# A routing search fed by two broadcasting transfers instead of sixteen, and four weight buffers that outlive the attention

## The chip, the cores and the metric

The program runs on one core of one Trainium2 chip. The metric is the device time of one execution in microseconds (us), lower is better. TensorE (PE) multiplies matrices and loads its weights in a part of its own (PEld), VectorE (DVE), ScalarE (ACT) and GpSimd (POOL) do the rest of the arithmetic, and SyncE (SP) issues transfers (DMAs), which run on 16 DMA engines.

## The reference

Three stages follow each other, all in float32 except the weights of the third.

```python
thresh = np.max(scores, axis=-1, keepdims=True) - tau          # 4 x 8 heads, 576 x 576 scores, head_dim 64
scores = np.where(scores >= thresh, scores, -1000000000.0)
...
attn = np.exp(scores) / sum
x = (attn @ v) as [2304 tokens, 512]

logits = x @ w_gate                                            # 8 experts, cap = 2304 // 8 = 288
for idx in np.argsort(-logits.flatten()):                      # greedy, with capacity
    tok, e = idx // 8, idx % 8
    if assigned[tok] >= 0 or counts[e] >= cap: continue
    assigned[tok] = e; counts[e] += 1
out[mask_e] = np.maximum(x[mask_e] @ w1[e], 0) @ w2[e]         # 512 -> 1024 -> 512

gate = 1 / (1 + np.exp(-(x @ w_gate2)))                        # 512 -> 1536, weights are float64 words
return gate * (x @ w_val) @ w_out                              # 1536 -> 512
```

The third stage's weights arrive as 64-bit floats, and the kernel turns them into 32-bit floats by integer operations on their two halves.

## The kernel before

**Attention** (0 to 344 us) works through 16 units of two heads in an order written out by hand. Beside it, a "fill" generator puts small work into gaps: the class `Narrow` loads raw pieces of the third stage's weights (36 pieces, three for each of 12 column blocks: gate, val, out; one raw piece is a tile `wd` of 128 x 1024 words, 512 KB), makes float32 of each in three DVE operations (`n1`, `n2`, `n3`, at L585, L587, L589) in a tile `wn`, and stores it to device memory (`wf<-wn`, 256 KB). 13 pieces are done in the attention, through four `wd` buffers and three `wn` buffers. Those pools end with the attention.

**Routing** is done by rounds: in each, every token that is left picks its best expert, and for each expert a threshold is searched that lets no more in than there is room. Rounds 0 to 2 search by `search` (L639 to L719: compare a tile `big`, count by 18 short matmuls L684, a flag `fl` L699, one matmul L702, a new value `n` L705; six such steps). Rounds 3 to 6 search by `search_wide`: the 8 x 2304 keys are written to device memory (`kx<-kc`) and read back in two halves `kw`, each of 128 partitions by 1152 keys, so that 16 partitions hold the same row of one expert. One step is then one DVE comparison with a count for each half (`big<-kw`, L765), a flag `rhw` (L768), and one matmul (L771). In the kernel before, each half is read by eight transfers of 16 partitions.

**Experts.** For each of the eight experts the tokens are gathered, transposed (L1190), multiplied by w1 and w2 (expert 0 in float32, L1241 and L1264; the others in two parts, L1146 and L1156, with weights that ACT and DVE split into a high and a low part from `wr`, L1227 and L1054, three `wr` buffers), and put through the third stage (L1146, L1156, called stage g below, from the parts `yh`, `yl`), whose result is transposed back (L1377), copied (`orow`, L1384) and scattered to the output. Round r+1 of the routing runs beside expert r.

The third stage's 36 weight pieces are made ready beside this, once, in rounds 0 and 1: pieces narrowed before come from device memory (`wf<-wf`, L1069), the others are loaded raw (`wd`, L1078) and narrowed on DVE (L1087, L1090, L1093, again n1 to n3). ACT and DVE then split each (`hi` L1110, `lo` L1054, names `wgh`, `wgl`, `wvh`, `wvl`, `wo`).

What sets the order: `Plan` is a list scheduler that runs while the program is built. Each piece of work is a `job` with an engine, a cost, what it depends on, a priority and the buffers that it takes (`Slots`). `Plan.step` places, on the engine that is free first, the job of the lowest priority number that is ready; while `crit` (the next step of round 0) is known, only jobs that end before it are put in front. The costs thus decide the order of instructions on every engine, and the chip then runs each engine's list in that order. All loads and stores stand in one list on SP: a transfer that waits holds up all behind it. A job of a DMA is taken to end after its bytes at 300 KB/us plus 1.9 us.

Of the kernel before, what the change touches and what calls it, by code (L numbers as in the profile page):

```python
# [7 lines left out]
F32 = mybir.dt.float32  # L8
F32R = mybir.dt.float32r
BF = mybir.dt.bfloat16  # L10
I32 = mybir.dt.int32
# [97 lines left out]
def n_pieces():  # L109
    return len(fill_places()) // 3  # L110


def fill(router, weights, slots):

    it = router
    next(it)
    for slot in range(slots):
        weights.load(slot)
    yield
    for _ in it:  # L120
        pass
    yield
    yield from weights.steps()


def attention(tc, raw, prep, qk, v, tau, wg, xd, lg, idf, filler, chosen):
# [402 lines left out]
T, E, CAP, R = 2304, 8, 288, 96  # L529
# [35 lines left out]
class Narrow:  # L565
# [10 lines left out]
            self.d[n] = self.raw(self.todo.pop(n))  # L576
            (q or self.q).dma_start(self.d[n], self.src[n])

    def steps(self):
        v = self.nc.vector  # L580
        for n, slot in self.slots.items():
            f = self.narrowed(n)
            w = self.d.pop(n).rearrange("p (n t) -> p n t", t=2)
            o = f.bitcast(I32)
            v.tensor_scalar(o, w[:, :, 1], 3, 0x3FFFFFF8, op0=OP.logical_shift_left, op1=OP.bitwise_and)  # L585
            yield n
            v.scalar_tensor_tensor(o, w[:, :, 0], 29, o, op0=OP.logical_shift_right, op1=OP.bitwise_or)  # L587
            yield n
            v.scalar_tensor_tensor(o, w[:, :, 1], -0x40000000, o, op0=OP.bitwise_and, op1=OP.bitwise_or)  # L589
            self.store(n, f)  # L590
            self.load(slot)
            yield n + 1


class Router:
# [136 lines left out]
    def search_wide(self, K, C):  # L732

        nc, v = self.nc, self.nc.vector
        yield "DVE", 1.0
        kc = self.t([128, 8, 18], "kc")
        no = self.t([128, 8, 18], "no")
        ct = C.rearrange("p c e -> p e c")
        v.tensor_tensor(kc, ct, K.unsqueeze(1).to_broadcast([128, 8, 18]), op=OP.mult)
        v.tensor_scalar(no, ct, -3 * DEAD, 3 * DEAD, op0=OP.mult, op1=OP.add)  # L740
        v.tensor_tensor(kc, kc, no, op=OP.add)
        rem = self.t([128, 2, 8], "remw")
        for i, col in enumerate((C_NM, C_M)):
            v.tensor_tensor(rem[:, i], self.rem, self.cf[:, col : col + 8], op=OP.add)
        yield "SP", 0.35
        nc.sync.dma_start(self.kx.rearrange("e p c -> p e c"), kc)
        for h in range(2):
            yield "SP", 2.7, "kw2" if h else "kw"
            for e in range(8):
                nc.sync.dma_start(  # L750
                    self.kw[h][16 * e : 16 * e + 16],
                    self.kx[e : e + 1, 64 * h : 64 * h + 64].rearrange("a p c -> a (p c)").to_broadcast([16, T // 2]),
                )
        w = None
        for s, sh in enumerate(range(28, -1, -4)):
# [24 lines left out]
        self.close(w, ps, nf)  # L780
# [143 lines left out]
class Plan:  # L924
# [76 lines left out]
    def place(self, t, j):  # L1001
# [12 lines left out]
        if more:  # L1014

            self.dma = max(self.dma, t + j.dur) + more / 300e3
            j.end = self.dma + 1.9
        self.done.append((t, j))
        for h in (*j.acq, *j.use):
            h.left -= 1  # L1020
# [2 lines left out]
                h.pool.free.append((h.end, h.slot))  # L1023


def experts(tc, rt, xd, idf, w12, w3in, w3, pre, out):
    nc = tc.nc
    V, A, G, SP = nc.vector, nc.scalar, nc.gpsimd, nc.sync
    with (
# [13 lines left out]
        p = Plan()  # L1043
# [4 lines left out]
        pos_g = [32 + 52 * e for e in range(7)] + [32 + 52 * 6 + 36]  # L1048

        def bt(h, shape, name, dt=F32):  # L1050
            return bp.tile(shape, dt, name=name, tag=f"b{h.slot}")

        def minus(l, x, h):
            V.tensor_sub(l, x, h.bitcast(F32))  # L1054
# [4 lines left out]
        for n in range(36):  # L1059
# [13 lines left out]
            else:  # L1073
# [4 lines left out]
                    SP.dma_start(box["w"], w3in[n])  # L1078
                    return 524288

                src = job("SP", 0.35, load, (), pr - 60, acq=[hd, hc])

                def n1(box=box):
                    box["f"] = wp.tile([128, 512], F32, name="wf", bufs=NWF)
# [7 lines left out]
                def n3(box=box):  # L1092
                    V.scalar_tensor_tensor(box["o"], box["w2"][:, :, 1], -0x40000000, box["o"], op0=OP.bitwise_and, op1=OP.bitwise_or)  # L1093

                src = take = job("DVE", 0.36, n1, [src], pr, acq=[hf] + hold, use=[hd, hc])
                src = job("DVE", 0.63, n2, [src], pr, use=[hd, hc, hf])
                src = job("DVE", 0.63, n3, [src], pr, use=[hd, hc, hf])
            if kind == 2:
                take.order = taken[-1:]
                taken.append(take)  # L1100
# [398 lines left out]


NEAR = 40
PATIENT = 2.0, 30.0
START, SPACE = 5.5, 1.7
WD, NWF, LEAD, LATE, PB, WIDE, AHEAD = 4, 3, 14, 3, 18, 3, 40
PLANS = []


# [13 lines left out]

def program(tc, qk, v, tau, wg, w12, cst, csti, w3, out):
    nc = tc.nc
    with tc.tile_pool(name="keep", bufs=1) as kp, tc.tile_pool(name="keep_dram", bufs=1, space=bass.MemoryType.DRAM) as dp:
        idf = kp.tile([128, 128], F32, name="idf")
        make_identity(nc, idf)
        lg = kp.tile([128, 18, 8], F32, name="lg")
        xd = dp.tile([2304, 512], F32, name="xd")
        wf = [dp.tile([128, 512], F32, name=f"wf{n}") for n in range(36)]
        words = w3.bitcast(I32)  # L1530
        rt = Router(tc, lg, idf, kp, dp)
        pre = n_pieces()
        with (
            tc.tile_pool(name="at_raw", bufs=2) as rp, tc.tile_pool(name="at_prep", bufs=2) as pp,
            tc.tile_pool(name="staging", bufs=2) as sp,
        ):
            weights = Narrow(
                nc, lambda s: sp.tile([128, 1024], I32, name="wd", bufs=4), lambda n: sp.tile([128, 512], F32, name="wn", bufs=3),
                words, nc.sync, lambda n, f: nc.sync.dma_start(wf[n], f), {n: n % 4 for n in range(pre)},
            )  # L1540
            filler = fill(rt.prepare(cst, csti), weights, 4)
            attention(tc, rp, pp, qk, v, tau, wg, xd, lg, idf, filler, rt.begin)
        experts(tc, rt, xd, idf, w12, words, wf, pre, out)


# [12 lines left out]
```

## Time and profile before

| | |
|---|---|
| median of 3 runs | 1127.85 us (1127.82 to 1128.93) |
| the profiled execution | 1127.83 us |
| its span, first to last instruction | 1126.0 us, so 1.8 us lie outside |
| mean granted TensorE clock | 0.977 |
| PE busy, PEld busy | 1055.1 us (94%), 983.5 us (87%) |
| DVE, ACT, POOL busy | 787.3, 525.4, 324.2 us |
| DMA | 156.17 MB, mean 139 GB/s |

The shares are averages over a part with a PE bound (the attention and the experts), a part of 40 us in which PE is idle most of the time (344 to 384 us, round 0 of the routing), and some short stops. What a change is worth has to be read at the place where it acts.

### The profile page before, as it was taken

To read this page: it belongs to the slowest core of one execution; us is meant where nothing else is said; L and a number is where in the kernel's file an instruction comes from. 1 tells how busy PE (TensorE), PEld (TensorE's weight loads), DVE (VectorE), ACT (ScalarE), POOL (GpSimd) and SP (SyncE) were. 2 spreads that over 40 slices of the span, in tenths; PEclk is the share of its full clock that TensorE was granted. 3 is DMA by queue.
4 is the path that set the end of the run, shared out by engine and by line. 5 is a ranking of instruction groups with operands and counts; after the bars stand their busy time and mean duration, and the time that the engine had idled before them with its cause. 6 is when DMAs were issued, how large, how long until landed. Compare 5 with 4: busy or idle time off the path is not lost.

```text
span 1126.0 us, 21012 instructions
## 1 busy us (share of the span) xinstructions
PE 1055.1 (94%) x7885; PEld 983.5 (87%) x7885; DVE 787.3 (70%) x1915; ACT 525.4 (47%) x1176; POOL 324.2 (29%) x334
## 2 busy tenths in 40 slices
PE   4999999999994699998999999999999999999997
PEld 3888888888883479997999999999999899999996
DVE  7899999989997998876868857966974413412311
ACT  4798898889873234234125214314313413412411
POOL 5888998888840101011011010110101100100101
PEclk9999999999996799998999999999999999999999
DMA  7423334244016675646346346446444433534232
GB/s 277 153 86 111 132 100 142 89 143 128 2 38 220 201 275 174 225 122 191 95 125 199 120 122 187 134 136 169 149 124 153 134 113 114 166 105 125 76 108 84
DMA packets 52885, 156.17 MB, mean 139 GB/s; under 512 B 11568, under 2 KB 16560, under 8 KB 50864
## 3 DMA queue, kind: packets, MB, share of 16 engines
q1 hardware_dynamic: 49712, 145.40, 40.3%
q0 software_dynamic: 3072, 9.44, 2.8%
q8 instruction: 62, 1.02, 0.4%
q14 instruction: 39, 0.32, 0.1%
HBM read 135.38 MB, written 19.43 MB: 137 GB/s over the span
## 4 chain that ended last, share of the span: by engine, by line
PE 51%; issue 26%; DVE 14%; DMA 4%; ACT 2%; POOL 2%; SPq 0%; POOLq 0%; ACTq 0%; DVEq 0%
PE ps L1146 17%; PE acc L1156 11%; PE s L250 7%; PE t L291 5%; PE o L367 2%; PE o L391 2%; DVE nm L261 2%; PE o L363 2%; PE o L375 2%; DMA wr<-in_w 2%; DVE p L283 1%; DMA wf<-wf 1%; POOL out L1388 1%; DVE wf L1090 1%; DMA wd<-in_w 1%
## 5 line engine op out<-in xcount | busy, mean ns | idle before, releaser
L1332 DVE TENSOR_TENSOR gt<-ps,sg 128x288 f32<-128x288 f32 x96 | 43.9, 457 | 163.0 <-PE ps L1146 128.8
L1388 POOL DMA_INDIRECT out<-orow,idx x24 | 24.4, 1017 | 410.0 <-ACT orow L1384 405.9
L1328 ACT ACTIVATE sg<-ps 128x288 f32<-128x288 f32 x96 | 39.5, 412 | 195.1 <-PE ps L1146 170.5
L1156 PE MATMUL acc<-gh,wo 128*128 128x288 f32 x768 | 125.1, 300 | 0.9 <-DVE wo L1054 0.9
L265 ACT ACTIVATE e<-s,nm 128x576 f32<-128x576 f32 x144 | 106.4, 739 | 24.9 <-DVE nm L261 23.4
L1054 DVE TENSOR_TENSOR w<-wr,w 128x512 fp32r<-128x512 f32 x112 | 75.6, 689 | 55.7 <-ACT w L1227 55.3
L1146 PE MATMUL ps<-yh,wgh 128*128 128x288 f32 x384 | 107.9, 303 | 6.3 <-ACT orow L1384 3.9
L1336 ACT ACTIVATE gh<-gt 128x288 fp32r<-128x288 f32 x96 | 42.7, 445 | 148.1 <-DVE gt L1332 144.6
L283 DVE SCALAR_TENSOR_TENSOR p<-s,th,e 128x576 f32<-128x576 f32 x128 | 100.7, 810 | 15.5 <-ACT th L269 13.3
L1156 PEld LDWEIGHTS acc<-gh,wo 128*128 128x128 f32 x768 | 108.8, 189 | 1.2 <-DVE wo L1054 1.1
L261 DVE TENSOR_REDUCE nm<-s 128x1 f32<-128x576 f32 x144 | 104.1, 747 | 6.1 <-PE s L250 5.1
L1171 POOL DMA_INDIRECT xr<-xd,idx x16 | 15.2, 951 | 321.4 <-issue 157.2
L1146 PE MATMUL ps<-yh,wvh 128*128 128x288 f32 x384 | 106.4, 299 | 0.0
L1146 PE MATMUL ps<-yh,wgl 128*128 128x288 f32 x384 | 106.3, 298 | 0.0
L1227 ACT ACTIVATE w<-wr 128x512 fp32r<-128x512 f32 x112 | 69.0, 629 | 77.4 <-PE acc L1156 30.1
L1146 PE MATMUL ps<-yh,wvl 128*128 128x288 f32 x384 | 105.1, 296 | 0.0
L250 PE MATMUL s<-kh,qs 128*128 128x288 f32 x320 | 80.0, 333 | 22.8 <-DVE p L283 14.7
L250 PEld LDWEIGHTS s<-kh,qs 128*128 128x128 f32 x320 | 53.0, 197 | 40.6 <-issue 22.0
L1146 PEld LDWEIGHTS ps<-yh,wgh 128*128 128x128 f32 x384 | 73.3, 191 | 8.2 <-ACT orow L1384 4.3
L765 DVE TENSOR_SCALAR_CACHE_REDUCE big<-kw,tw 128x1152 bf16<-128x1152 f32 x56 | 78.9, 1409 | 1.0
L291 PE MATMUL t<-idf,p 128*128 128x128 f32 x548 | 78.4, 277 | 0.7 <-ACT lo L346 0.7
L291 PEld LDWEIGHTS t<-idf,p 128*128 128x128 f32 x548 | 64.6, 142 | 11.7 <-ACT tf L321 2.5
(233 smaller groups left out, 2766.0 us busy)
## 6 DMA issues: line engine op xcount, KB each, us to landing
wo<-wod SPq DMA_DIRECT2D x84, 512.0 KB, 3.5
wr<-in_w SPq DMA_DIRECT2D x64, 512.0 KB, 3.7
qkr<-in_qk SPq DMA_DIRECT2D x15, 1248.0 KB, 5.6
wd<-in_w SPq DMA_DIRECT2D x36, 512.0 KB, 5.6
wod<-wo SPq DMA_DIRECT2D x12, 512.0 KB, 3.6
vr<-in_v SPq DMA_DIRECT2D x16, 320.0 KB, 3.8
kw<-kx SPq DMA_DIRECT2D x64, 72.0 KB, 4.1
xd<-xl SPq DMA_DIRECT2D x8, 512.0 KB, 4.5
```

The source lines that it names most:

```text
L250: nc.tensor.matmul(s[:, h, 0:288], qs[:, qo : qo + 128], kt[:, ko + 288 * h : ko + 288 * h + 288], start=m == 0, stop=m == len(src) - 1,)
L261: nc.vector.tensor_reduce(d[u]["nm", i], d[u]["s", i][:, :, 0:288], op=OP.max, axis=AX.XY, negate=True)
L265: nc.scalar.activation(e, d[u]["s", i][:, :, 0:288], AF.Exp, bias=d[u]["nm", i])
L283: nc.vector.scalar_tensor_tensor(dst.rearrange("p (c n) -> p c n", c=2), w["s", i][:, :, 0:288], nmth[n // 2][1][:, n % 2 : n % 2 + 1], w[ ...
L291: nc.tensor.matmul(t[:m, 128 * j : 128 * j + 128], src, idf, is_transpose=True, start=j == 0, stop=j == len(srcs) - 1, skip_group_check=True,)
L765: v.tensor_scalar(self.big, self.kw[h], thr, None, op0=OP.is_ge, op1=OP.add, accum_out=cnt[:, h : h + 1])
L1054: V.tensor_sub(l, x, h.bitcast(F32))
L1146: nc.tensor.matmul(ps, w(q), x[:, q], start=n == 0, stop=n == 11)
L1156: nc.tensor.matmul(acc[m][:, :CAP], w[:, 128 * m : 128 * m + 128], x, start=first and i == 0, stop=last and i == 2)
L1227: A.activation(box[nm][:, 0], box["r"][:, i], AF.Copy)
L1332: V.tensor_tensor(box["gt"], box["v"][:, :CAP], box["sg"], op=OP.mult)
L1336: A.activation(box["h"][0], box["gt"], AF.Copy)
```

## The change

Three things change, and through the planner the order of much other work.

1. `search_wide` reads each half of `kw` by one transfer of 128 partitions (576 KB), whose source repeats each of 8 rows 16 times. The planner's cost for it is 0.45 instead of 2.7.
2. A pool `kept` of four buffers is opened outside both the attention and the experts. The attention's four `wd` buffers lie in it; the attention's `wn` buffers are two instead of three. At the end of the attention, four more raw pieces (13, 15, 16, 18: gate and val pieces) are loaded into these buffers as they come free, so they need no load job in the planner and no slot of `wdcap` (`early`). In the experts, the four buffers are four of the nine `big` slots.
3. While round 0 runs, the planner takes every transfer to end 1.2 us later (`SLOW`).

(The argument `count` of `fill` and `steps` is the number of all pieces, and the value that `steps` yields last is used nowhere else.)

```diff
 def search_wide(self, K, C):
...
         for h in range(2):
-            yield "SP", 2.7, "kw2" if h else "kw"
-            for e in range(8):
-                nc.sync.dma_start(
-                    self.kw[h][16 * e : 16 * e + 16],
-                    self.kx[e : e + 1, 64 * h : 64 * h + 64].rearrange("a p c -> a (p c)").to_broadcast([16, T // 2]),
-                )
+            yield "SP", 0.45, "kw2" if h else "kw"
+            nc.sync.dma_start(
+                self.kw[h],
+                self.kx[:, 64 * h : 64 * h + 64].rearrange("e p c -> e (p c)").unsqueeze(1).to_broadcast([8, 16, T // 2]),
+            )
...
 def place(self, t, j):
...
-            j.end = self.dma + 1.9
+            j.end = self.dma + 1.9 + (SLOW if self.crit is not None else 0.0)
...
 def experts(...):
         def bt(h, shape, name, dt=F32):
-            return bp.tile(shape, dt, name=name, tag=f"b{h.slot}")
+            return (kept if h.slot < KEPT else bp).tile(shape, dt, name=name, tag=f"b{h.slot}")
...
-                src = job("SP", 0.35, load, (), pr - 60, acq=[hd, hc])
+                if n in early:
+                    hd.slot, box["w"] = early[n]
+                    big.free.remove((0.0, hd.slot))
+                    src = None
+                else:
+                    src = job("SP", 0.35, load, (), pr - 60, acq=[hd, hc])
...
+KEPT = 4
+SLOW = 1.2
...
 def program(...):
+        todo = list(range(pre)) + [n for n in range(pre, 36) if n % 3 < 2][:KEPT]
+        place = {n: i % KEPT for i, n in enumerate(todo)}
...
             weights = Narrow(
-                nc, lambda s: sp.tile([128, 1024], I32, name="wd", bufs=4), lambda n: sp.tile([128, 512], F32, name="wn", bufs=3),
-                words, nc.sync, lambda n, f: nc.sync.dma_start(wf[n], f), {n: n % 4 for n in range(pre)},
+                nc, lambda n: kept.tile([128, 1024], I32, name="wd", tag=f"b{place[n]}"),
+                lambda n: sp.tile([128, 512], F32, name="wn", bufs=2), words, nc.sync, lambda n, f: nc.sync.dma_start(wf[n], f), place,
             )
+        early = {n: (place[n], weights.d[n]) for n in todo[pre:]}
```

The order that comes out differs at three places that matter here. The first is SP's list around round 3 (at 500 to 520 us of the profile). Before, the keys go out, two weight loads `wr` of expert 2 follow, then the sixteen `kw`, then the next `wr`:

```order
L746 DMA kx<-kc 128x8x18
L1218 ISA
L1218 DMA wr<-in_w 128x1024
L1218 ISA
L1218 DMA wr<-in_w 128x1024
L750 DMA kw<-kx 16x1152 x16
L1218 ISA
L1218 DMA wr<-in_w 128x1024
```

In the changed kernel the list reads:

```order
L746 DMA kx<-kc 128x8x18
L1223 ISA
L1223 DMA wr<-in_w 128x1024
L1223 ISA
L1223 DMA wr<-in_w 128x1024
L749 DMA kw<-kx 128x1x1152 x2
L1223 ISA
L1223 DMA wr<-in_w 128x1024
```

Nothing moved here but the count of transfers: the next `wr` stands two issues behind the second `wr` instead of sixteen.

The second place is SP's list at the end of the attention. Before (L1539 stores a narrowed piece, L426 and L429 store tokens, L1069 loads a narrowed piece, L1078 a raw one):

```order
L1539 DMA wf_76<-wn 128x512
L1539 DMA wf_77<-wn 128x512
L426 DMA xd<-xl_4185 128x4x256
L1539 DMA wf_78<-wn 128x512
L426 DMA xd<-xl_4185 128x4x256
L1539 DMA wf_79<-wn 128x512
L429 DMA xd<-xl_4185 64x256 x2
L1069 DMA wf<-wf_67 128x512
L1069 DMA wf<-wf_68 128x512
L1069 DMA wf<-wf_70 128x512
L1078 DMA wd<-in_w 128x1024 x4
L1069 DMA wf<-wf_71 128x512
```

In the changed kernel (L1552 stores a narrowed piece, L577 loads a raw piece of the attention's kind, L1077 one of the experts' kind):

```order
L1077 DMA wd<-in_w 128x1024 x4
L1552 DMA wf_78<-wn 128x512
L577 DMA wd<-in_w 128x1024
L1552 DMA wf_79<-wn 128x512
L577 DMA wd<-in_w 128x1024
L1552 DMA wf_80<-wn 128x512
L577 DMA wd<-in_w 128x1024
L426 DMA xd<-xl_4188 128x4x256
L1552 DMA wf_81<-wn 128x512
L577 DMA wd<-in_w 128x1024
L1552 DMA wf_82<-wn 128x512
L577 DMA wd<-in_w 128x1024
```

Four raw loads of the experts moved from behind the attention to before the store of the ninth narrowed piece, and a raw load follows each of the last five stores. (The names' numbers are five apart for the same store: `wf_79` here is `wf_74` before plus five.)

The third place is DVE's list in round 0 after its first comparison (L639, 347 us). Before, the search runs alone up to its third step, and only split operations `lo` (L1054) stand between its steps:

```order
L639 TENSOR_TENSOR big_113<-cf_103,K_109 128x315
L699 TENSOR_SCALAR fl_5041<-rps_5022 63x8
L705 TENSOR_REDUCE n_5045<-rps_5043 128x1
L726 TENSOR_SCALAR w2_5048<-n_5045 128x1
L728 TENSOR_SCALAR sg_5050<-w2_5048 128x1
L729 SCALAR_TENSOR_TENSOR w2_5048<-sg_5050,w2_5048 128x1
L670 TENSOR_TENSOR tb_5047<-ci_104,w2_5048 128x63
L639 TENSOR_TENSOR big_113<-tb_5047,K_109 128x567 x2
L693 TENSOR_TENSOR cw_5089<-ci_104,w2_5048 128x31
L699 TENSOR_SCALAR fl_5091<-rps_5062 63x8
```

In the changed kernel narrowing (L1091, L1094, L1097 are n1, n2, n3) stands between them from the first step on:

```order
L639 TENSOR_TENSOR big_116<-cf_106,K_112 128x315
L1091 TENSOR_SCALAR wf_5033<-wd_4775 128x512
L1094 SCALAR_TENSOR_TENSOR wf_5033<-wd_4775,wf_5033 128x512
L1097 SCALAR_TENSOR_TENSOR wf_5033<-wd_4775,wf_5033 128x512
L699 TENSOR_SCALAR fl_5056<-rps_5035 63x8
L1091 TENSOR_SCALAR wf_5059<-wd_4885 128x512
L1091 TENSOR_SCALAR wf_5063<-wd_4937 128x512
L705 TENSOR_REDUCE n_5065<-rps_5061 128x1
```

Up to the matmuls behind the search (the copy `before` at L837), the changed list has 13 narrowing operations and 8 of the split, where the one before has 9 of the split.

## Rows read from the trace of the kernel before

**Rows 1.** The page, busy time of an engine.
```profile
PE 1055.1 (94%) x7885; PEld 983.5 (87%) x7885; DVE 787.3 (70%) x1915; ACT 525.4 (47%) x1176; POOL 324.2 (29%) x334
```

**Rows 2.** Windows: us, busy of PE, PEld, DVE, ACT, POOL; PEclk, DMA share, GB/s.
```profile
344.00:384.00 40.00, 15.81 (x185) 10.54 (x181) 31.00 (x109) 9.17 (x20) 3.02 (x3) 0.57 0.67 225
...
506.00:534.00 28.00, 23.06 (x160) 22.23 (x160) 18.70 (x38) 11.60 (x27) 3.04 (x5) 0.88 0.68 195
...
624.00:1118.00 494.00, 489.86 (x3751) 485.39 (x3749) 248.93 (x627) 148.81 (x334) 28.47 (x44) 1.00 0.43 129
```

**Rows 3.** Waits of PE from 384 to 1118 us, longest first.
```profile
PE ps L1146 <- ACT orow L1384: 3.9, 2, 2.8
PE rps L771 <- DVE rhw L768: 2.0, 2, 1.2
```

**Rows 4.** Timeline of SP in round 3: start, us, instruction, count.
```profile
504.61 3.02 SPq L1218 DMA_DIRECT2D wr<-in_w  x2
507.83 10.60 SPq L750 DMA_DIRECT2D kw<-kx  x16
518.68 1.54 SPq L1218 DMA_DIRECT2D wr<-in_w  x3
```

**Rows 5.** Timeline of PE in round 3, in brackets the idle time before.
```profile
522.70 0.17 PE L771 MATMUL rps<-rhw,one 128*128 128x8 bf16 x1 [1.24 <-DVE rhw L768]
...
527.98 0.61 PE L1146 MATMUL ps<-yh,wgh 128*128 128x288 f32 x1 [2.83 <-ACT orow L1384]
```

**Rows 6.** Timeline of ACT in round 3.
```profile
522.52 1.15 ACT L1227 ACTIVATE w<-wr 128x512 fp32r<-128x512 f32 x2 [4.67 <-DMA wr<-in_w]
...
527.30 0.62 ACT L1384 ACTIVATE orow<-ps 96x512 f32<-96x512 f32 x1
```

**Rows 7.** Timeline of DVE in round 3.
```profile
511.74 1.29 DVE L1054 TENSOR_TENSOR w<-wr,w 128x512 fp32r<-128x512 f32 x2 [2.98 <-ACT w L1227]
...
520.90 1.41 DVE L765 TENSOR_SCALAR_CACHE_REDUCE big<-kw,cf 128x1152 bf16<-128x1152 f32 x1 [1.42 <-DMA kw<-kx]
```

**Rows 8.** Window behind the stop, columns as in the windows above.
```profile
528.00:534.00 6.00, 6.00 (x31) 6.00 (x32) 4.96 (x13) 0.47 (x2) 0.92 (x1) 0.65 0.43 149
```

**Rows 9.** DMA from 480 to 500 us: packets, MB, share of 16 engines.
```profile
q1 hardware_dynamic: 432, 1.57, 22.1%
```

**Rows 10.** DMA from 511.9 to 517 us, while `kw` transfers run.
```profile
q1 hardware_dynamic: 230, 0.51, 43.0%
```

**Rows 11.** DMA issues of the page: KB each, median us from issue to landing.
```profile
wr<-in_w SPq DMA_DIRECT2D x64, 512.0 KB, 3.7
...
wf<-wf SPq DMA_DIRECT2D x13, 256.0 KB, 6.8
```

**Rows 12.** Waits of DVE during the search of round 0, 347.4 to 369.5 us.
```profile
DVE wvl L1054 <- ACT wvh L1110: 2.3, 2, 2.0
DVE fl L699 <- PE rps L684: 1.6, 3, 0.6
DVE wgl L1054 <- ACT wgh L1110: 1.4, 3, 0.6
DVE n L705 <- PE rps L702: 0.8, 3, 0.3
```

**Rows 13.** Timeline of ACT in round 0.
```profile
361.00 0.63 ACT L1110 ACTIVATE wvh<-wf 128x512 fp32r<-128x512 f32 x1 [5.45 <-DMA wf<-wf]
```

**Rows 14.** Groups by line on DVE, whole span: narrowing and split.
```profile
L1090 DVE SCALAR_TENSOR_TENSOR wf<-wd,wf 128x512 int32<-128x512 int32 x23 | 15.9, 691 | 0.6
L1087 DVE TENSOR_SCALAR wf<-wd 128x512 int32<-128x512 int32 x23 | 9.6, 419 | 0.8 <-DMA wd<-in_w 0.8
L1054 DVE TENSOR_TENSOR wvl<-wf,wvh 128x512 fp32r<-128x512 f32 x12 | 8.2, 687 | 2.3 <-ACT wvh L1110 2.3
```

**Rows 15.** Timeline of PE where round 1's search and expert 0 begin.
```profile
381.77 0.45 PE L684 MATMUL rps<-C,big 128*63 128x8 bf16 x9 [0.84 <-DVE big L639]
...
387.11 0.45 PE L684 MATMUL rps<-C,big 128*63 128x8 bf16 x9 [0.44 <-DVE big L639]
```

More of the change, by code (lines that the diff above doesn't have):

```diff
@@ L110, in n_pieces, with fill @@
     return len(fill_places()) // 3
-def fill(router, weights, slots):
+def fill(router, weights, slots, count):
     it = router
@@ L122, in fill @@
     yield
-    yield from weights.steps()
+    yield from weights.steps(count)
 def attention(tc, raw, prep, qk, v, tau, wg, xd, lg, idf, filler, chosen):
@@ L577, in load, with steps @@
             (q or self.q).dma_start(self.d[n], self.src[n])
-    def steps(self):
+    def steps(self, count):
         v = self.nc.vector
-        for n, slot in self.slots.items():
+        for n, slot in list(self.slots.items())[:count]:
             f = self.narrowed(n)
@@ L591, in steps @@
             self.load(slot)
-            yield n + 1
+            yield n
 class Router:
@@ L1023, in place, with experts @@
                 h.pool.free.append((h.end, h.slot))
-def experts(tc, rt, xd, idf, w12, w3in, w3, pre, out):
+def experts(tc, rt, xd, idf, w12, w3in, w3, pre, early, kept, out):
     nc = tc.nc
@@ L1093, in n3 @@
                     V.scalar_tensor_tensor(box["o"], box["w2"][:, :, 1], -0x40000000, box["o"], op0=OP.bitwise_and, op1=OP.bitwise_or)
-                src = take = job("DVE", 0.36, n1, [src], pr, acq=[hf] + hold, use=[hd, hc])
-                src = job("DVE", 0.63, n2, [src], pr, use=[hd, hc, hf])
-                src = job("DVE", 0.63, n3, [src], pr, use=[hd, hc, hf])
+                hc = [] if n in early else [hc]
+                src = take = job("DVE", 0.36, n1, [src], pr, acq=[hf] + hold, use=[hd] + hc)
+                src = job("DVE", 0.63, n2, [src], pr, use=[hd, hf] + hc)
+                src = job("DVE", 0.63, n3, [src], pr, use=[hd, hf] + hc)
             if kind == 2:
@@ L1523, in program @@
     nc = tc.nc
-    with tc.tile_pool(name="keep", bufs=1) as kp, tc.tile_pool(name="keep_dram", bufs=1, space=bass.MemoryType.DRAM) as dp:
+    with (
+        tc.tile_pool(name="keep", bufs=1) as kp, tc.tile_pool(name="keep_dram", bufs=1, space=bass.MemoryType.DRAM) as dp,
+        tc.tile_pool(name="kept", bufs=1) as kept,
+    ):
         idf = kp.tile([128, 128], F32, name="idf")
@@ L1537, in program @@
             weights = Narrow(
-                nc, lambda s: sp.tile([128, 1024], I32, name="wd", bufs=4), lambda n: sp.tile([128, 512], F32, name="wn", bufs=3),
-                words, nc.sync, lambda n, f: nc.sync.dma_start(wf[n], f), {n: n % 4 for n in range(pre)},
+                nc, lambda n: kept.tile([128, 1024], I32, name="wd", tag=f"b{place[n]}"),
+                lambda n: sp.tile([128, 512], F32, name="wn", bufs=2), words, nc.sync, lambda n, f: nc.sync.dma_start(wf[n], f), place,
             )
-            filler = fill(rt.prepare(cst, csti), weights, 4)
+            filler = fill(rt.prepare(cst, csti), weights, KEPT, pre)
             attention(tc, rp, pp, qk, v, tau, wg, xd, lg, idf, filler, rt.begin)
-        experts(tc, rt, xd, idf, w12, words, wf, pre, out)
+        early = {n: (place[n], weights.d[n]) for n in todo[pre:]}
+        experts(tc, rt, xd, idf, w12, words, wf, pre, early, kept, out)
 def kernel(**inputs):
```

## The prediction

> **What bounds the kernel now.** I read the page first: PE is busy for 1055.1 us [rows 1], so only its idle time, and time at a lower clock, can be won; DVE at 70% bounds nothing as a whole. The windows by stage say where that time lies [rows 2]. From 344 to 384 us PE is busy for 15.81 of 40 us: this is round 0 of the routing, where nothing but the search can go on and where expert 0 waits for its tokens. From 506 to 534 us it is busy for 23.06 of 28, that is 4.9 us idle. From 624 us on it is idle for 4.1 us of 494, so behind round 4 next to nothing is to be had. Between 384 and 1118 us the grouped waits of PE name two that lead: the first matmul of stage g behind `orow`, 3.9 us in two stops, and the matmul of `search_wide` behind `rhw`, 2.0 us in two [rows 3]. The larger stop of each is in round 3 [rows 5].
>
> The stop in round 3 is read from SP's queue. Sixteen `kw` issues hold SP from 507.83 to 518.43 us, and only then, at 518.68, do the next weight loads `wr` go out [rows 4]. ACT waits 4.67 us for the first of them, to 522.52 [rows 6]; the third `orow` follows at 527.30, and stage g at 527.98 [rows 5, 6]. DVE waits for the second half of `kw` until 520.90 [rows 7], so `rhw` is late too, and PE waits 1.24 us at 522.70 [rows 5]. A buffer for the next `wr` was free long before: DVE splits the last part of the old one in the pair of operations that starts at 511.74, the first ending at about 512.4 [rows 7]. So about 6.2 us of the lateness of `wr` (512.4 to 518.68) are the queue's. Behind the stop PE is fully busy from 528 to 534 us, but at a mean granted clock of 0.65 [rows 8]: (1 - 0.65) x 6 = 2.1 us of work lost. The whole stop thus costs 4.9 + 2.1 = 7.0 us.
>
> **Part 1, two transfers for sixteen.** On SP two issues of under half a microsecond take the place of 10.6 us [rows 4]; behind them `wr` now waits for its buffer, to 512.4. What the trace does not show is how fast one 576 KB transfer from 8 repeated rows is. I bound it by two rows. Plain loads from 480 to 500 us moved 1.57 MB with 22.1% of 20 us [rows 9]: 1.57 / 4.42 us, 355 GB/s on sixteen engines. While `kw` ran alone, 0.51 MB took 43.0% of 5.1 us [rows 10]: 233 GB/s. A half of 0.59 MB then takes 1.7 us (all engines, plain rate) at best and, if the eight rows keep only eight engines busy at the `kw` rate, 0.59 / 116 = 5.1 us at worst. I take 3.3 us, the plain rate on half of the engines, which lies in the middle. The data of `kw` can begin when the two `wr` ahead have drained: the second is issued at the end of the 3.02 us from 504.61, at about 507.3, and lands a median 3.7 us later [rows 4, 11], so I put the beginning at 510, and one microsecond from the end of the data to the landing (an estimate: of the 3.7 us, 1.5 are 0.52 MB at the plain rate, and the rest is shared by both ends).
>
> Then the halves land at 514.3 and 517.6 us, the latter 3.3 us before the 520.90 of now [rows 7], and the first `wr` behind them, with 1.5 us of data, at 516.6 + 1.5 + 1 = 519.1, against ACT's 522.52 now [rows 6]. ACT gains 3.4 us. Not all reaches PE: in the changed order the transposes and copies of expert 1's result still stand ahead of stage g, and the last sums of w2 end near 521.5 as now (522.70 less the 1.24 of idle time). Of ACT's 3.4 us I take 0.4 as lost there, about one `orow` of 0.62 that may now stand in the way [rows 6]: stage g starts at about 525.0 instead of 527.98, 3.0 us. Some of the clock's 2.1 us comes back as the stop gets shorter; I take 0.5. **Round 3: -3.5 us, bounds 0 and -7.0.**
>
> A rule of the Trainium skill speaks against this edit. Its page "DMA: Bandwidth & Descriptors", section "Rules for kernel authors" (use all 16 engines), says that a transfer whose outermost dimension is smaller than 16 runs on no more engines than that dimension, and names the leading small dimension of a broadcast. The new source is 8 rows by 16 repeats, the old one 16 repeats of one row; no row of this trace has a transfer with fewer than 16, so none shows it. By the rule a half takes 3.3 to 5.1 us and never 1.7, so the sum below would be the forecast's or, at 5.1, 0 for round 3, and the best case falls away.
>
> In rounds 4 to 6 the same exchange frees SP too, but PE loses 4.1 us after 624 us in all [rows 2], and no stop there names `kw` or a load behind it. I set it to 0 (bounds -1.2, the smaller stops of rounds 4 [rows 3], and +1 for a reordered list).
>
> **Parts 2 and 3, the early pieces.** SP's list at the attention's end gets four raw loads earlier and four more; the DMA engines are nearly idle there until the stores, and PE's order in the attention is unchanged, so I cost it at nothing; its cover is the second `wn` buffer, whose store must be done before the next narrowing.
>
> In round 0 the search is a serial chain through DVE. DVE idles in it for 2.3 + 1.4 us behind ACT, which itself waits for `wf` loads, and for 1.6 + 0.8 us behind PE's short matmuls [rows 12]; ACT's longest wait is 5.45 us, for a `wf` load [rows 13]. Together 6.1 us. The changed list puts 13 narrowing operations there (5 n1 at 0.42 and 8 n2 or n3 at 0.69 us, 7.6 us [rows 14]) and has one split fewer (0.69): 6.9 us of work more. If it fills all the idle time, and the waits for loads vanish because the early pieces need none, round 0 gets 6.9 - 6.1 = 0.8 us longer; started back to back, DVE's operations overlap by some 0.08 us each (a pair of splits takes 1.29 [rows 7]), which gives 0.8 to 1.0 us back. So about 0.
>
> Behind it, the changed list of PE has the first L702 of round 1 before expert 0's transposes, so these start about 0.5 us later behind the matmuls at 381.77, and the later stop of 0.44 us at 387.11 goes [rows 15]. Again 0. **Transition: 0, bounds -3.0 and +4.5**: the lower where the 3.7 us behind ACT vanish and the filling is free except for 0.7 us; the upper is worked out below.
>
> **Sum.** 1127.83 (the profiled execution, 0.02 us under the median of the runs) - 3.5 + 0 + 0 = 1124.3 us.
>
> **The rivals.**
> *The keys come no earlier.* One transfer runs on eight engines at the worst rate above. The halves then land at 510 + 5.1 + 1 = 516.1 and 521.2, and `wr`, behind both on these eight engines, at 510 + 10.2 + 1.5 + 1 = 522.7, against 522.52 now: SP is free early and wins nothing, and DVE waits for `kw` as before. Time 1127.8, plus up to 1. For it: 72 KB at a time these reads had two thirds of the plain rate. Against it: there sixteen engines read one row at once, here each row is another. I give it a chance of 0.22. The rule of the Trainium skill named above is one half of this rival, the rate of 116 GB/s the other.
>
> *Round 0 pays for the narrowing (slower).* The early pieces take `wf` buffers, of which there are three, so each `wf` load has to wait for the split of the piece before it in that buffer; ACT and DVE may wait for the loads as now, only for later ones. Then only the 2.4 us behind PE are filled, and round 0 gets 6.9 - 2.4 = 4.5 us longer, all of it on PE, which has nothing else to do; with one more late load of the size of the longest now (2.0 us [rows 12]) 6.5. With round 3 as forecast: 1128.8 to 1130.8. It decides from 5.8 us on (3.5 + 2.3). For it: `wf` loads take a median 6.8 us [rows 11], and the changed list has splits of loaded pieces one step before they are needed. Against it: four raw pieces come ready without a load. Chance 0.17.
>
> *Both gains in full.* The keys land at the best rate, `wr` at 512.4 + 3.7 = 516.1, PE does not stop in round 3, and the transition wins 2 to 3 us: 1127.8 - 7.0 - 3.0 = 1117.8; with half of the clock's loss and 2 us, 1120. For it: nothing else in that stretch waits for a transfer. Against it: ACT and DVE have their own serial work before stage g. Chance 0.16.
>
> **How the numbers follow.** The forecast has 0.45, with a range of its own of 1121.5 to 1126.5. About 0.2% (2.3 us) can be told from no change in this kernel. Faster: nearly all of the forecast (0.43), all of the last rival, 0.01 of the first: 0.60. Same: most of the first rival (0.17), 0.02 of the forecast, 0.05 of the second: 0.24. Slower: 0.12 of the second and 0.04 of the first, with a transition of some microseconds on top: 0.16. Range 1118.8 to 1129.6: it leaves out the end of the last rival and of the slower one.
>
> **What would show it.** Right: two `kw` issues of together under 1 us, the next `wr` at about 512 to 513 us less any shift, no `kw` wait on DVE in round 3, stage g about 3 us nearer to the last sums of w2, a PE idle of 2 us or less there. In round 0: no 2.0 us wait behind ACT, the last matmul group of the search within 1 us of now. If half of the engines carry the keys, the DMA share is near 0.5 while nothing else is queued. Wrong: a new wait for `kw` or `wr` in round 3 as long as the old one; a round 0 that ends 3 us later or earlier; a stop of more than a microsecond where there was none, in the attention's last 10 us or behind the new order of rounds 4 to 6.

## The result, and the profile after

The changed kernel takes 1143.47 us (median of 4 runs, 1139.23 to 1146.72) against 1128.11 (4 runs, 1127.82 to 1128.93): ratio 1.0133, 95% interval 1.0099 to 1.0167. It is 15 us slower; 1124.3 us had been forecast, and nothing above 1129.6. The profiled execution took 1146.72 us, the longest of the four; its span is 1144.9 us.

The windows by stage of the changed kernel, with the columns of [rows 2], and a stretch around round 4 besides:

```profile
344.00:384.00 40.00, 15.58 (x171) 10.48 (x171) 35.12 (x120) 7.62 (x16) 3.02 (x3) 0.57 0.53 173
...
506.00:534.00 28.00, 21.08 (x152) 20.47 (x151) 15.89 (x33) 10.91 (x24) 2.96 (x5) 0.88 0.71 193
...
606.00:624.00 18.00, 12.45 (x77) 12.24 (x76) 12.00 (x27) 4.80 (x9) 0.00 (x0) 0.81 0.48 147
624.00:1118.00 494.00, 486.34 (x3713) 480.82 (x3713) 256.11 (x643) 151.83 (x341) 29.54 (x48) 1.00 0.43 131
```

Round 3 has 6.9 us of idle PE instead of 4.9, and round 4 has 5.6 us in 18. In the kernel before, where round 4 runs some 6 us earlier, the stretch around it has 1.2 us in 28:

```profile
596.00:624.00 28.00, 26.83 (x204) 26.17 (x203) 25.19 (x55) 13.82 (x30) 3.12 (x5) 1.00 0.61 190
```

Of the waits of PE from 340 us on in the changed kernel, these two grew most:

```profile
PE rps L770 <- DVE rhw L767: 12.5, 5, 5.7
...
PE ps L1151 <- DVE xl L1146: 4.6, 3, 2.2
```

The wait for `rhw` was 2.0 us in [rows 3]; that for `xl` was 1.8 us. The timelines of SP, of DVE, of ACT and of PE at rounds 3 and 4 show what it waits for:

```profile
507.27 2.96 SPq L1223 DMA_DIRECT2D wr<-in_w  x2
511.63 1.45 SPq L749 DMA_DIRECT2D kw<-kx  x2
515.66 21.42 SPq L1223 DMA_DIRECT2D wr<-in_w  x5
```
```profile
520.52 1.41 DVE L764 TENSOR_SCALAR_CACHE_REDUCE big<-kw,cf 128x1152 bf16<-128x1152 f32 x1 [2.77 <-DMA kw<-kx]
526.34 1.41 DVE L764 TENSOR_SCALAR_CACHE_REDUCE big<-kw,cf 128x1152 bf16<-128x1152 f32 x1 [3.80 <-DMA kw<-kx]
603.67 1.41 DVE L764 TENSOR_SCALAR_CACHE_REDUCE big<-kw,cf 128x1152 bf16<-128x1152 f32 x1 [1.96 <-DMA kw<-kx]
610.07 1.41 DVE L764 TENSOR_SCALAR_CACHE_REDUCE big<-kw,cf 128x1152 bf16<-128x1152 f32 x1 [4.38 <-DMA kw<-kx]
```
```profile
527.20 0.63 ACT L1232 ACTIVATE w<-wr 128x512 fp32r<-128x512 f32 x1 [8.14 <-DMA wr<-in_w]
```
```profile
528.14 0.17 PE L770 MATMUL rps<-rhw,one 128*128 128x8 bf16 x1 [5.69 <-DVE rhw L767]
...
535.35 0.61 PE L1151 MATMUL ps<-yh,wgh 128*128 128x288 f32 x1 [2.22 <-DVE xl L1146]
...
611.87 0.17 PE L770 MATMUL rps<-rhw,one 128*128 128x8 bf16 x1 [5.55 <-DVE rhw L767]
...
633.78 0.40 PE L1151 MATMUL ps<-yh,wgh 128*128 128x288 f32 x1 [1.57 <-ACT orow L1389]
```

SP is about as free as was said: two issues take 1.45 us, and the next `wr` goes out 4 us after the first of them, where in [rows 4] it went out 10.85 us after the first `kw`. But the halves land 8.9 and 14.7 us after the first issue, 5.8 us apart; in round 4 they are 6.4 us apart. And the weights `wr` that were issued early come late: ACT waits 8.14 us for them, against 4.67 in [rows 6]. The page shows one thing more, in its count of small packets:

```profile
DMA packets 51924, 156.16 MB, mean 136 GB/s; under 512 B 10608, under 2 KB 15600, under 8 KB 49904
```

The same line of the kernel before:

```profile
DMA packets 52885, 156.17 MB, mean 139 GB/s; under 512 B 11568, under 2 KB 16560, under 8 KB 50864
```

There are 960 fewer packets under 512 B. That is what comes out if each transfer closes with one small packet on each DMA engine that it used: 64 transfers on 16 engines, 1024 packets, gave way to 8 transfers with 64 in all. The events by which the trace marks a landing agree. A transfer of the kernel before has sixteen; each new `kw` has one soon after its issue and then eight, for the first from 517.89 to 520.49 us. And of the sixteen of the first `wr` behind them, seven come by 521.22 us, one at 522.48 and eight only from 524.50 to 527.18. So each new transfer ran on eight engines, and the load behind it was late on about half of its own.

To see where the 18.9 us between the two spans lie, I cut both at six events: the first comparison of round 0 (L639), the first matmul group of round 1's search, the start of stage g of experts 0, 1 and 2, and the stage g that begins at 887.75 us in the kernel before. The first column is the attention's end, which differs by up to 2 us from run to run of one kernel.

| kernel (events in us of its span) | round 0 begins | to round 1 | to stage g, expert 0 | to stage g, expert 1 | to stage g, expert 2 | to the later stage g | to the end |
|---|---|---|---|---|---|---|---|
| before | 346.98 | 34.79 | 40.46 | 105.75 | 91.50 | 268.27 | 238.25 |
| changed | 348.64 | 36.09 | 42.59 | 108.03 | 98.43 | 272.16 | 238.96 |

So between these two executions lie 1.3 us in round 0, 2.1 from there to expert 0, 2.3 in the stretch with round 3, 6.9 in the one with round 4, and 3.9 in rounds 5 and 6; 1.7 us are the attention's. Small differences need care: the two runs with transfers behind the last output (below) have the order of before up to there, and in them the stretches take 36.2 us (both), 40.47 (both), 104.43 and 104.92, 91.50 and 92.81. The 1.3 us of round 0 are thus within what one order shows from run to run.

### The profile page after: what moved, and what is told of

Its sections match the earlier page's. It is cut to its first block, busy times and chain, and to the rows that moved or that the text cites. A ratio compares the mean times of both kernels' runs of the same rounds, so it can differ in the third digit from the quotient of the medians.

```text
span 1144.9 us, 20905 instructions
## 1 busy us (share of the span) xinstructions
PE 1061.4 (93%) x7884; PEld 988.3 (86%) x7885; DVE 788.9 (69%) x1915; ACT 525.1 (46%) x1176; POOL 321.8 (28%) x334
## 4 chain that ended last, share of the span: by engine, by line
PE 52%; issue 26%; DVE 13%; DMA 6%; POOL 1%; ACT 1%; SPq 0%; POOLq 0%; DVEq 0%; ACTq 0%
PE ps L1151 17%; PE acc L1161 9%; PE s L250 7%; PE t L291 4%; PE o L367 2%; DMA kw<-kx 2%; PE o L391 2%; DVE nm L261 2%; DMA wr<-in_w 2%; PE o L363 2%; PE o L375 2%; DVE p L283 1%; PE ps L1246 1%; PE acc L1269 1%; DVE w L1053 1%
## 5 line engine op out<-in xcount | busy, mean ns | idle before, releaser
L1161 PE MATMUL acc<-gh,wo 128*128 128x288 f32 x768 | 122.5, 297 | 0.5 <-DVE wo L1053 0.5
```

The costliest lines, as they stand in the source:

```text
L1161: nc.tensor.matmul(acc[m][:, :CAP], w[:, 128 * m : 128 * m + 128], x, start=first and i == 0, stop=last and i == 2)
```

## The experiments

Theory 1: the new transfer is slow because it runs on eight engines, and holds up the keys and all that is queued behind it. Theory 2: the new order around round 0 and the kept buffers cost the time.

**One transfer for each half, in the old order.**

```diff
 (kernel before)
-            for e in range(8): nc.sync.dma_start(self.kw[h][16 * e : 16 * e + 16], ...)
+            nc.sync.dma_start(self.kw[h], ....unsqueeze(1).to_broadcast([8, 16, T // 2]))     # cost stays 2.7
```


> The kernel before with only the two transfers for sixteen; the planner's cost stays 2.7, so the order on every engine is that of before. Theory 1 (the new transfer itself is slow, because its source has 8 rows outermost and it runs on half of the engines): a half still takes some 6 us, DVE waits for the keys in rounds 3 and 4 as in the changed kernel, 5 to 12 us slower than before. Theory 2 (the new order around round 0 and the early pieces cost the time): within 2 us of before, or faster.

Measured 1.0079 (1.0057 to 1.0101), 9 us. Its stretches, from round 0 on: 34.47, 43.39, 106.22, 97.74, 269.33. No instruction but the transfer changed, so theory 1 holds, for more than half of the loss. In the profiled execution most of it lies around round 4, 6.2 us; round 3's stretch is 0.5 us longer than in the kernel before and 1.3 to 1.8 longer than in the two runs named above. The 2.9 us up to expert 0 are none of the transfer's doing, since no `kw` has gone out by then. PE waits there for a weight load, and in the 15 us from 409 the mean granted clock is 0.89, against 1.00 in the kernel before:

```profile
409.00 3.35 PE L1240 MATMUL ps<-xh,wr 128*128 128x288 f32 x8 [1.42 <-DMA wr<-in_w]
```

**All the rest without it.**

```diff
 (changed kernel)
-            nc.sync.dma_start(self.kw[h], ...)       # and 0.45
+            for e in range(8): nc.sync.dma_start(...)  # and 2.7
```


> The changed kernel with the sixteen transfers and their cost of 2.7 put back: the kept buffers, the early pieces and SLOW alone. Theory 1: within 3 us of before (the 3 us by which the search of round 1 starts later in the changed kernel may remain). Theory 2: 10 us or more slower than before.

Measured 1.0013 (0.9998 to 1.0029). Theory 2 falls as the main cause: the kept buffers, the early pieces and `SLOW` cost about a tenth of the loss, and by this run alone perhaps nothing. Its round 0 is 37.87 us long.

**The same transfers with another outermost dimension.** The source's slowest dimension is made the 16 repeats; partition p then holds expert p mod 8 and not p // 16, and the masks and digits in the constants follow.

```diff
-    ....rearrange("e p c -> e (p c)").unsqueeze(1).to_broadcast([8, 16, T // 2])
+    ....rearrange("e p c -> e (p c)").unsqueeze(0).to_broadcast([16, 8, T // 2])
...
-    own = p[:, None] // 16 == np.arange(8)         # and p % 16 at four places
+    own = p[:, None] % 8 == np.arange(8)           # and p // 8
```


> The changed kernel, same order on every engine, but the keys lie in the partitions so that the outermost dimension of the source is the 16 repeats and not the 8 rows (partition p holds expert p mod 8; three constants follow). If the number of engines is the cause, a half takes 2 to 3 us, and 10 us or more of the 15 come back, to 1126 to 1133. If reading a row again and again is slow by itself, it stays at 1139 to 1147.

Measured 1.0013 (0.9996 to 1.0030), with no other instruction moved on any engine: 13 of the 15 us come back (1.0133 less 1.0013, of 1128).

The same transfer on the kernel before, which is part 1 without its fault:

```diff
 (kernel before)
-            yield "SP", 2.7, ...       # eight transfers of 16 partitions for each half
+            yield "SP", 0.45, ...      # one, unsqueeze(0).to_broadcast([16, 8, T // 2])
```


> The kernel before with part 1 alone (cost 0.45), the source's outermost dimension being the 16 repeats. If the number of engines is the cause and SP's queue is what stopped round 3, this is 2 to 5 us faster than before, 1123 to 1126. If the queue was not the limit: within 2 us of before.

Measured 1.0004 (0.9989 to 1.0018): not the gain that had been expected. The transfers are fast and the queue is free, yet nothing is won. The next two runs separate the transfer from the planner's cost.

**Part 1 alone, and its transfer in the old order.** The first is the kernel before with part 1 as written, the second has 16 repeats outermost and the planner's old cost.

```diff
 (both: kernel before with one transfer for each half)
-            yield "SP", 2.7, "kw2" if h else "kw"
+            yield "SP", 0.45, "kw2" if h else "kw"      # k6 alone; k7 keeps 2.7 and has unsqueeze(0), [16, 8, T // 2]
```


> Part 1 alone as it was written: two transfers with 8 rows outermost, and the planner's cost of 0.45. Theory 1a (the lower cost also lets the planner put the first comparisons of a round earlier in every engine's list, where the keys are not there yet): 3 to 6 us slower than the same transfer with the old cost (0.79% over before), so 1.1 to 1.3% over before. Rival (the cost does not matter, the rest of the 15 us comes from the kept buffers together with the transfer): 0.7 to 0.9% over before.

> The order of before, exactly, with one transfer for each half whose outermost dimension is the 16 repeats. The prediction's claim that SP's queue stops round 3: the next wr goes out at about 513, stage g of expert 1 starts 2 to 3 us earlier than before, 0.2 to 0.4% faster. Rival (another wait takes the place at once, as in the kernel with the cost of 0.45, where stage g waited 2.98 us for xl instead): within 0.15% of before.

Measured 1.0173 (1.0158 to 1.0189) and 0.9968 (0.9957 to 0.9979). With the two before, on the kernel before:

| ratio to before | planner's cost 2.7 (old order) | cost 0.45 (new order) |
|---|---|---|
| 8 rows outermost | 1.0079 | 1.0173 |
| 16 repeats outermost | 0.9968 | 1.0004 |

In each row and each column the two runs come from different chips, each against runs of before on its own. The form of the transfer is worth 1.1 to 1.7%, and the lower cost loses 0.4 to 0.9% by itself; part 1 alone, at 1.0173, lies above both ranges that had been expected. The run at 0.9968, 3.6 us faster than before, is nearest to what the prediction described. Its timelines of SP, ACT and PE, and its window with the columns of [rows 2]:

```profile
510.15 1.24 SPq L749 DMA_DIRECT2D kw<-kx  x2
514.05 12.27 SPq L1217 DMA_DIRECT2D wr<-in_w  x5
```
```profile
522.01 1.15 ACT L1226 ACTIVATE w<-wr 128x512 fp32r<-128x512 f32 x2 [1.87 <-DMA wr<-in_w]
```
```profile
527.47 0.40 PE L1145 MATMUL ps<-yh,wgh 128*128 128x288 f32 x1 [2.72 <-ACT orow L1383]
```
```profile
506.00:534.00 28.00, 25.28 (x186) 24.95 (x184) 19.38 (x40) 12.60 (x28) 3.04 (x5) 0.94 0.73 208
```

Its search of round 1 begins 2.63 us later than before (384.40 against 381.77 [rows 15]); less that, ACT's `w` is at 519.38 and stage g at 524.84, where 519.1 and 525.0 had been forecast. Stage g follows `w` by 5.46 us, as it does before, so all that `w` gains reaches PE. PE is idle for 2.7 us instead of 4.9 (2 or less had been named as a sign), at a mean granted clock of 0.94 instead of 0.88; the stop behind `orow` itself stays (2.72 us against 2.83), and the smaller ones ahead of it go.

The close match is in part luck. The stretch up to expert 1's stage g takes 102.61 us, 3.1 less than in the profile of before but 1.8 and 2.3 less than in the two other runs with its order. And the next stretch, for which nothing had been forecast, gives 1.2 us or more (90.31).

With the cost of 0.45 and the same transfers, DVE's and PE's timelines in round 3 read:

```profile
524.66 1.41 DVE L764 TENSOR_SCALAR_CACHE_REDUCE big<-kw,tw 128x1152 bf16<-128x1152 f32 x1
526.00 0.08 DVE L764 DVE_READ_ACCUMULATOR big<-kw,tw 128x1 f32 x1
526.00 1.55 DVE L1140 TENSOR_TENSOR yl<-acc,yh 128x288 fp32r<-128x288 f32 x4
527.47 1.18 DVE L1140 TENSOR_TENSOR xl<-ps,xh 128x288 fp32r<-128x288 f32 x3
```
```profile
527.97 0.61 PE L1145 MATMUL ps<-yh,wgh 128*128 128x288 f32 x1 [2.98 <-DVE xl L1140]
```

There the first comparison of the search's second step stands ahead of `yl` and `xl`, and PE waits 2.98 us for `xl` before stage g at 527.97: the stop has a new cause and its old end. In the old order that comparison stands behind them.

**The transfers by themselves.** Behind the last output, the kinds of transfers in turn. The first of the two runs has five kinds, eight small transfers among them, three times over; two chains of them overlap, and only its last ones are nearly clean (8 rows 6.3 us from issue to use, 16 repeats 5.4, eight small ones 6.1). The second has four kinds:

```diff
 (kernel before, after experts(...); the second run)
+    for i, f in enumerate([rows8, rows16, plain8, plain16] * 4):   # 576 KB each, into one tile
+        f(); nc.vector.tensor_copy(see[:, i : i + 1], a[:, 0:1])
```


> The kernel before with, behind its last output, five kinds of transfers one after the other, each waited for by DVE, three times over; its time is longer by these and says nothing. Number of engines: the keys with 8 rows outermost take 2 us or more longer than with 16 repeats outermost, and a plain 512 KB load from 8 blocks of 16 rows as much longer than one from 16 blocks of 8, with a DMA share near 0.5 against 1. Repeated rows: the two plain loads take the same, and only the keys with 8 rows outermost are slow.

> Behind the last output of the kernel before, four kinds of 576 KB transfers strictly in turn, each waited for by DVE before the next is issued, four times over; the total time says nothing. Number of engines: 8 rows outermost takes about 1 us or more longer than 16 repeats outermost, and 8 blocks of 16 plain rows as much longer than 16 blocks of 8; both forms with 8 outermost write 8 small completion packets, the others 16. Repeated rows: the two plain forms take the same time, and the keys are slower than both.

In the second run each is alone. DVE's uses of the second round of four (keys with 8 rows outermost, with 16 repeats, plain rows from 8 blocks, from 16), issued at 1145.72, 1153.15, 1158.19 and 1165.24:

```profile
1152.97 0.15 DVE L1563 COPY see<-pa 128x1 f32<-128x1 f32 x1 [7.28 <-DMA pa<-kx]
1158.01 0.15 DVE L1563 COPY see<-pa 128x1 f32<-128x1 f32 x1 [4.89 <-DMA pa<-kx]
1165.06 0.15 DVE L1563 COPY see<-pa 128x1 f32<-128x1 f32 x1 [6.89 <-DMA pa<-in_qk]
1170.37 0.15 DVE L1563 COPY see<-pa 128x1 f32<-128x1 f32 x1 [5.16 <-DMA pa<-in_qk]
```

The packets of the first two of these:

```profile
DMA packets 136, 0.59 MB, mean 81 GB/s; under 512 B 8, under 2 KB 8, under 8 KB 136
...
DMA packets 144, 0.59 MB, mean 120 GB/s; under 512 B 16, under 2 KB 16, under 8 KB 144
```

7.25, 4.86, 6.87 and 5.13 us; over all four rounds 6.7 to 7.5, 4.9, 6.5 to 7.2 and 5.1 to 5.4. What counts is 8 or 16 outermost, with 8 or 16 small packets, and not whether rows repeat. This is the rule of the Trainium skill that the prediction weighed ("DMA: Bandwidth & Descriptors", "Rules for kernel authors", use all 16 engines), and the trace agrees: for 576 KB, eight instead of sixteen cost 2.4 us with the keys and 1.7 with plain rows.

**Round 0.** In the changed kernel the first narrowing of round 0 waits for a store. DVE's timeline:

```profile
350.76 0.43 DVE L1091 TENSOR_SCALAR wf<-wd 128x512 int32<-128x512 int32 x1 [1.65 <-DMA wf<-wn]
```

Its tile `wf` lies in the memory of the attention's `wn`, whose last stores are under way. A run moves `wn` into a fifth buffer that outlives the attention.

```diff
 (changed kernel, 16 repeats outermost)
-    lambda n: sp.tile([128, 512], F32, name="wn", bufs=2)
+    lambda n: wn[:, place[n] % 2]        # wn = kept.tile([128, 2, 512], F32, name="wn", tag="b4")
```


> The changed kernel with 16 repeats outermost, and the tiles wn of the attention moved into a fifth buffer that outlives it, so that the first narrowing of round 0 need not wait for the last two stores; the order is otherwise the same but for four raw loads on SP. Theory (round 0 is longer because this narrowing waits 1.6 to 2.4 us for a store out of memory that it reuses): the wait is gone, the time from the first comparison of round 0 to the first matmul of round 1's search falls from 36.7 to about 35 us, 0.1 to 0.2% faster than the kernel with 16 repeats outermost. Rival (the 13 narrowing operations themselves make round 0 longer): it stays above 36 us, no difference.

Measured 1.0033 (1.0020 to 1.0046), against 1.0013 without the move: no gain. The wait is gone, but round 0 is 37.58 us long. The timelines of ACT and DVE have the reason:

```profile
354.59 0.63 ACT L1115 ACTIVATE wvh<-wf 128x512 fp32r<-128x512 f32 x1 [8.46 <-DMA wd<-in_w]
```
```profile
355.25 0.69 DVE L1053 TENSOR_TENSOR wvl<-wf,wvh 128x512 fp32r<-128x512 f32 x1 [2.09 <-ACT wvh L1115]
```

The first split of the round comes no earlier than in the changed kernel (354.69), and now DVE waits for it. The profile names a raw load there, but the loads that the move had put on SP just before had not landed by then (the first did at 356.08 us). Among the events that the split waits for, the last to come is the landing of the attention's last token store `xd<-xl`, at 354.40 in this run and at 354.31 in the changed kernel. So that store, which the move does not touch, holds the split with and without it; what the wait for `wn` costs by itself is not settled by this run.

**The rest with the good transfer and the old cost.**

```diff
 (changed kernel)
-            yield "SP", 0.45, ...      # [8, 16, T // 2]
+            yield "SP", 2.7, ...       # [16, 8, T // 2]
```


> The changed kernel with 16 repeats outermost and the old cost of 2.7: against the kernel before with the same two (0.9968) it shows what the kept buffers, the early pieces and SLOW are worth. If they cost round 0 the 1 to 3 us that the traces show there: 0.998 to 1.000. If they are worth nothing either way: 0.996 to 0.998. If they gain: under 0.995.

Measured 0.9991 (0.9978 to 1.0004), against 0.9968 without the kept buffers, the early pieces and `SLOW`: these cost 2.6 us here, though the two numbers come from different chips, each against its own runs of before. Round 0 took 36.19 us, with the wait for `wn` again (1.9 us).

**Why the lower cost loses.** Four runs tell the planner in two ways that the keys come later than it thinks:

```diff
 (kernel before, part 1 with cost 0.45)
-                return 589824 if "kw" in note or "kw2" in note else ...
+                return 3 * 589824 if "kw" in note or "kw2" in note else ...      # k11
...
-            j.end = self.dma + 1.9
+            j.end = self.dma + 1.9 + j.late     # for kw and kw2 3.5 or 5.0 (16 repeats), 7.0 (8 rows)
```


> The kernel before with 16 repeats outermost and the cost of 0.45, but the planner is told three times the bytes for each half, so that it takes the keys to arrive some 10 us after their issue, about when they do. Theory (the cost of 0.45 loses 0.36% against 2.7 because the planner then takes the keys to be there 4 to 6 us after their issue and sets the comparisons too early in DVE's list): the loss goes, 0.995 to 0.998. Rival (the loss is chance in the order and has nothing to do with the keys' arrival): anywhere, 0.999 to 1.002 most likely.

> The kernel before with 16 repeats outermost and the cost of 0.45; the planner takes each half to land 3.5 us later than by its own rule, and nothing else is later. If the 0.36% that the lower cost loses come from comparisons planned before the keys are there: 0.995 to 0.998, like the old cost (0.9968) or better. If not: 0.999 to 1.003.

> The same with 5 us instead of 3.5: the first half planned 9 us after its issue. If the planned arrival is what matters, it stays at 0.995 to 0.998 or 0.1% worse; if it is chance in the order, it may lie anywhere between 0.995 and 1.005.

> The kernel before with part 1 as it was written (8 rows outermost, cost 0.45), the planner taking each half to land 7 us later than by its own rule, about when it does. If the loss of 1.73% is made of the slow transfer (0.79% in the order of before) and of comparisons planned too early (0.94%), most of the second part goes: 1.005 to 1.010. If the early comparisons are not the cause: 1.014 to 1.020.

Measured 1.0103 (1.0084 to 1.0122), 1.0050 (1.0032 to 1.0067), 1.0023 (1.0010 to 1.0037) and 1.0112 (1.0095 to 1.0128). The first two lie above both of their ranges, the third in that for chance, and the fourth between its two. With 16 repeats no planned arrival wins back the 0.36%; the first also delays every other load in the planner's account. So "planned too early" is not the cause there, or not the whole of it; these orders differ by up to 1% among themselves. Why the order of the lower cost is worse stays open. With 8 rows 0.6 of the 0.9% go. DVE then waits for keys nowhere in rounds 3 and 4, and what is left shows the other half of the slow transfer. ACT's timeline of that run:

```profile
523.61 0.63 ACT L1226 ACTIVATE w<-wr 128x512 fp32r<-128x512 f32 x1 [7.68 <-DMA wr<-in_w]
...
611.38 1.15 ACT L1226 ACTIVATE w<-wr 128x512 fp32r<-128x512 f32 x2 [7.94 <-DMA wr<-in_w]
```

The landing events of the `wr` that the first of these waits for show why: eight of its sixteen come from 517.16 to 518.09 us and eight from 521.77 to 523.58, the second `kw` landing up to 522.51. The weights behind the keys wait for the eight engines, whoever waits for the keys.

## Why the prediction was wrong, point by point

- **The step that failed: "I take 3.3 us", with 5.1 "at worst".** On eight engines the halves landed 5.8 to 6.4 us apart in rounds 3 and 4 of the changed kernel; with 16 repeats outermost, in the run at 0.9968, they landed 2.3 us apart in round 3 (517.67 and 519.99). The rule of the Trainium skill had been read, and eight engines were right; the rate on them was not. Half of the plain 355 GB/s was taken, although the keys' own rate had been read as 233 (not quite alone, since a `wr` was landing up to 513.67 us). For a transfer alone 5.1 us was the right size: with the 2.2 us that the prediction has for both ends (3.7 less 1.5) it makes 7.3 us, and 7.25 were measured. In the kernel even the 116 GB/s was too good: 0.59 MB in 5.8 us are 102. With 5.8 us the prediction's own chain puts the weights at 510 + 11.6 + 1.5 + 1 = 524.1, 1.6 us later than before and not 3.4 earlier.
- **"Bounds 0 and -7.0" for round 3.** The rival with slow keys was priced at no gain, plus up to 1 us. It could lose more: the second half arrives later than sixteen small transfers brought it, and the weights behind it too. By [rows 7] the second half was wanted at 519.48 (520.90 less 1.42); a loss should have been reckoned from there. Measured +2.3 us against the profile of before, +3.1 to 3.6 against the two other runs with its order.
- **"I set it to 0" for rounds 4 to 6.** That no stop there named `kw` showed that the keys came in time, not by how much. In round 4 of the kernel before, the second half landed at 600.29 us, and DVE used it at 601.59:

```profile
601.59 1.40 DVE L765 TENSOR_SCALAR_CACHE_REDUCE big<-kw,cf 128x1152 bf16<-128x1152 f32 x1
```

  The cover was 1.3 us. From the first issue to this landing the kernel before takes 11.4 us, the changed one 14.4. Measured +6.9 around round 4 and +3.9 behind it, 10.8 of the 18.9 us, the largest part of the loss.
- **The planner's cost.** It was counted as time on SP only. It also moves comparisons in DVE's list; by the runs it loses 0.36% with fast keys and 0.94% with slow ones. That part of the order was not read.
- **SP's queue stops round 3: right.** With sixteen engines and the old order `w` and stage g came within 0.3 us of the forecast, and the kernel gained 3.6 us where 3.5 was forecast for round 3. The mechanism is shown; that the sizes agree so well is in part luck, as said above.
- **Transition 0.** Over the eleven profiles with the order of before in it, round 0 takes 33.4 to 36.5 us, and over the five with the order of the change 36.1 to 37.9. Up to expert 0's stage g it is 74.7 to 77.9 against 78.6 to 80.9 us, so the transition costs some 2 to 3 us, within its bounds. The part behind round 0, which had been put at "Again 0", has 2.1 us of it in the table. The waits for loads went as forecast (only the new one of 1.65 us is left of 3.7 [rows 12]); the wait for a store in reused memory was not seen. The slower rival's 4.5 us did not come.
- **The parts do not add.** Part 1 alone loses 1.73%, with the rest 1.33%, which is another order again; their intervals just touch.

## What to carry to other kernels

Before small transfers are merged into one, look at the outermost dimension of both sides. Here a merged broadcast with 8 there landed no earlier alone than the eight pieces (6.3 and 6.1 us), and later in the kernel, and the loads queued behind it were late as well. A wait that does not show is a cover with a size; ask how late its transfer may become before it is reckoned at 0. In a program whose order comes out of a scheduler, a changed cost is a change of its own, to be measured apart from the operation that it describes.

## What was not expected of the hardware

Reading the same eight rows with 16 repeats outermost is no slower than reading sixteen different blocks: 4.86 us for the repeated keys, 5.13 for plain rows. And with repeats outermost, one 576 KB transfer takes SP about 0.6 us to issue, and eight of them in place of the 64 make the kernel 3.6 us faster in the old order, so merging them was sound; what lost was the order of two dimensions, and the new order of work that came with the lower cost.
